# Four q turns moved from TensorE to DMA in an attention-and-MLP kernel

## The chip, the cores and the metric

The kernel runs on one core of one Trainium2 chip. The metric is the device time of one execution in microseconds, lower is better. It is about 1.8 us longer than the span of the profile of the same execution, which starts and ends with the first and last counted piece of work.

## The reference

Per batch and head there is a linear attention without softmax, then an RMS norm; then, over all heads together, a layer norm and a two-layer MLP with a residual.

```python
# 8 batches, 8 heads, 576 positions, head_dim 64; d_model 512, hidden 2048
kv  = np.einsum('bhsd,bhse->bhde', k, v)
out = np.einsum('bhsd,bhde->bhse', q, kv)
rms = np.sqrt(np.mean(out * out, axis=-1, keepdims=True) + 1e-06)
attn = out / rms * g_norm
x  = attn.transpose(0, 2, 1, 3).reshape(8, 576, 512)
xn = (x - mean(x)) / np.sqrt(var(x) + 1e-06) * g_ln
y  = x + np.maximum(xn @ w_ch1, 0.0) @ w_ch2
```

## The kernel before

The 8 x 576 rows are cut into tiles of 128 rows. Each batch has five slots: four of 128 rows, and a "last fifth" of 64 rows. A tile takes one slot (the last fifths of two batches share a tile). For every tile the kernel multiplies q by kv ("out"), and it reads q for that with head_dim on the partitions. So q has to be turned. There are two ways in the kernel. On TensorE a turn is four 128x128 identity matmuls and then one copy out of PSUM; as a DMA it is one transposing transfer on the SyncE (SP) queue. Before the change, all of batches 0 and 1 are turned on TensorE, and later batches by DMA, 20 blocks of 128x128 at a time.

```python
def q_turn_pe(b, t, h0, h1):                  # four blocks of slot t on TensorE
    # ... cut: tile and PSUM allocation
    for hp in range(h0 // 2, h1 // 2):
        nc.tensor.transpose(ps[:, hp, :],
            qp[b % 2][:, t, 2 * hp:2 * hp + 2, :].rearrange("p h d -> p (h d)"), identity)

def add_q_turn_pe(b, t, deps, key, eng, h0=0, h1=H):
    # ... plans the four transposes, then the copy from PSUM on VectorE or ScalarE

def q_turn_dma(b):                            # all 20 blocks of a batch
    att[b]["qT"] = work.tile([128, 20, 128], bf16, tag="qT", name="qT", bufs=3)
    nc.sync.dma_start_transpose(
        att[b]["qT"], qp[b % 2].rearrange("p t h d -> p (t h d)"))
```

The instructions are not written in the order of issue. Each step is put into a list with an engine, an estimated start and its dependences; a planner makes one order per engine from it, and each engine's instructions are put into the program in that order.

```python
# batch 1: q is copied into its turned-ready layout slot by slot on ScalarE, then turned
for t in range(5):
    # ... cut: key, and qperm = the ScalarE copy of slot t (t = 4 is loaded in place)
    add_q_turn_pe(1, t, [qperm, z1[1]], key + 1, ("DVE", "ACT")[t % 2])

# batch 2 and later: loads on GpSimd's queue, each behind a gate; then q copies (batch 2 alone) and a DMA turn
for t0, t1 in ((0, 2), (2, 4))[by_slot * 2:]:
    qperm.append(add("ACT", 0.85, 1.0, ok - 14, load["q", b][0:1] + [
        adone[b - 2]["qfree"]], lambda t0=t0, t1=t1: q_permute(nc.scalar, b, t0, t1)))
for x in kperm + qperm:
    x.lag = 4.0 if b == 2 else 6.0
turn = add_dma("SP", ok - 12, qperm + load["q", b] + (
    adone[b - 3].get("outs", []) if b >= 3 else []),
               lambda: q_turn_dma(b), 2.6e3, 1.0, occ=2.98, lat=0.25, tail=0.42)

# at the end: one order for all, and dummy matmuls in the early gaps of TensorE
order = run_plan()
# ... cut: idle[id(s)] = how many dummy matmuls go before TensorE step s
for s in order:
    if id(s) in idle:
        idle_mm(idle[id(s)])
    s.fn()
```

Three more names are used below. A "gate" is a one-column copy on GpSimd ("mark" in the profile) that reads a finished tile; the loads behind it in GpSimd's queue are issued after it (in the kernel before, one gate starts at 66.19 us, when the tile that it waits for has landed, and the load behind it at 66.65). "xT" is the normalized tile turned on TensorE and copied out of PSUM by ScalarE; the MLP's first layer ("m1") of a tile reads it. A "store" writes a finished tile of 256 KB to DRAM on the SP queue.

## Time and profile before

| | before |
|---|---|
| device time | 294.95 us, median of 3 (294.86 to 295.4) |
| PE busy | 283.4 us, 96% of the span |
| chain that ended last | on PE without a break from 25.53 to 290.36 us |
| q turns on PE that the change will remove | 4, of 0.22 us each |

These are the span, the busy times of the engines (with their number of instructions), and the chain by engine, from the page of the kernel before:

```profile
span 294.0 us, 5183 instructions
PE 283.4 (96%) x2061; PEld 161.6 (55%) x2061; DVE 166.1 (57%) x360; ACT 143.3 (49%) x288; POOL 65.5 (22%) x92
PE 90%; DMA 7%; POOL 1%; issue 1%; DVE 0%; POOLq 0%
```

TensorE (PE) is the bound: nine tenths of the chain are PE, and what the other engines do costs nothing as long as PE needn't wait for it. These are the four turns in question in the chain in order of time of the kernel before (start in us, length in us, what; the links between them are left out):

```profile
44.03 0.22 PE qT_ps L401 x4
47.07 0.22 PE qT_ps L401 x4
48.16 0.22 PE qT_ps L401 x4
52.05 0.22 PE qT_ps L401 x4
```

Each turn is a link of the chain, so each costs its 0.22 us in full. The next lines are from the DMA view of the kernel before for 36 to 52 us. The first has the queue, its packets, the MB moved and the share of the 16 engines' time; the others have the issues, with KB each and the median us from issue to landing.

```profile
q0 software_dynamic: 6651, 3.07, 146.9%
vb<-in_v_dram POOLq DMA_DIRECT2D x1, 512.0 KB, 14.1
qb<-in_q_dram POOLq DMA_DIRECT2D x1, 512.0 KB, 11.7
```

The loads keep the engines full throughout these 16 us. The q load of batch 2 ("qb") lands 11.7 us after its issue. Last, the timeline of the kernel before around this place (start, length, engine, line, what; in brackets idle time before it, and what ended it):

```profile
35.59 1.50 PE L429 MATMUL kv_ps<-vb,kp 96*128 96x128 bf16 x24
50.92 3.50 SPq L630 DMA_DIRECT2D out_dram<-x  x4
59.06 2.00 ACT L381 COPY qp<-qb 128x1024 bf16<-128x1024 bf16 x2
61.13 3.14 SPq L421 DMA_TRANSPOSE qT<-qp  x1
66.19 0.26 POOL L695 COPY mark<-qT 128x1 bf16<-128x1 bf16 x1 [9.32 <-DMA qT<-qp]
85.33 2.75 PE L598 MATMUL mm_ps<-xT,w 128*128 128x512 bf16 x12
```

ScalarE copies batch 2's q at 59.06 us without waiting (the load landed at 53.9). SP issues the DMA turn at 61.13, and GpSimd's one-column copy "mark", which waits for that turn only, starts at 66.19: about 5 us from issue to landing.

The first and last of these lines bound what I call the **stretch** below: from the start of batch 1's kv matmuls (35.59) to the first of the MLP's first-layer matmuls that is 128x512 (85.33; up to there they are 128x128), 49.74 us here. I call what follows block 2. All that the change adds to the DMA queues or takes from TensorE lies inside the stretch; of the rest of the change, the stores that are no longer split and batch 3's kv come later.

### The profile page before, as it was taken

Reading aid. Unit: us, or ns where it says so; the run is one execution under the profiler, and the core shown is the slowest. Engines: PE = TensorE matmul, PEld = TensorE weight load, DVE = VectorE, ACT = ScalarE, POOL = GpSimd, SP = SyncE. Lnnn points to the kernel's source line nnn. Section 1 sums busy time; section 2 is a strip of 40 time slices with the busy share of each in tenths; the row PEclk is TensorE's granted clock in tenths of the full one; section 3 lists DMA queues with packets and bytes.
Section 4 is the critical chain, followed back from the end, with each engine's and each line's share of the span. In section 5 each row is a group of like instructions: output and inputs, shape, how many; then the busy total and the mean of one; then the engine's idle time right before and its main releaser. Section 6 shows DMA issues by size and latency. Waiting matters only on the chain.

```text
span 294.0 us, 5183 instructions
## 1 busy us (share of the span) xinstructions
PE 283.4 (96%) x2061; PEld 161.6 (55%) x2061; DVE 166.1 (57%) x360; ACT 143.3 (49%) x288; POOL 65.5 (22%) x92
## 2 busy tenths in 40 slices
PE   3989999999999999999999999999999999999995
PEld 1879955977745445444544445444554444444444
DVE  1597048759876886557755775577557755420022
ACT  3268972987856612671267127611761177017400
POOL 8973230208209005403042316000000000000000
PEclk9999999999999999999999999999999999999999
DMA  7999999649989998991999699932201310220012
GB/s 98 181 199 205 203 199 192 173 91 108 189 173 95 167 132 159 174 212 56 171 116 146 115 142 133 178 96 89 56 18 54 91 54 18 56 85 22 0 74 73
DMA packets 107388, 35.21 MB, mean 120 GB/s; under 512 B 85603, under 2 KB 103395, under 8 KB 107364
## 3 DMA queue, kind: packets, MB, share of 16 engines
q0 software_dynamic: 72608, 18.35, 64.2%
q1 hardware_dynamic: 34516, 16.39, 23.6%
q8 instruction: 16, 0.26, 0.4%
q10 hardware_dynamic: 240, 0.13, 0.2%
q14 instruction: 8, 0.07, 0.1%
HBM read 36.70 MB, written 9.44 MB: 157 GB/s over the span
## 4 chain that ended last, share of the span: by engine, by line
PE 90%; DMA 7%; POOL 1%; issue 1%; DVE 0%; POOLq 0%
PE mm_ps L617 42%; PE mm_ps L598 33%; PE mm_ps L583 8%; DMA w<-in_moe_w_ch_dram 5%; PE kv_ps L429 3%; PE out_ps L452 3%; DMA vb<-in_v_dram 3%; PE xT_ps L533 1%; POOL kb L233 1%; PE qT_ps L401 0%; POOL vb L233 0%; DVE x L624 0%; POOL qp L254 0%; POOLq L943 0%
## 5 line engine op out<-in xcount | busy, mean ns | idle before, releaser
L617 PE MATMUL mm_ps<-w,m 128*128 128x512 bf16 (+2 forms) x608 | 130.3, 368 | 0.0
L598 PE MATMUL mm_ps<-xT,w 128*128 128x512 bf16 x448 | 100.8, 379 | 0.0
L605 ACT ACTIVATE m<-mm_ps 128x512 bf16<-128x512 f32 x112 | 66.8, 598 | 50.2 <-PE mm_ps L598 49.3
L617 PEld LDWEIGHTS <-m 128*128 128x128 bf16 x608 | 57.0, 98 | 59.6
L598 PEld LDWEIGHTS <-w 128*128 128x128 bf16 x448 | 43.1, 98 | 48.6
L624 DVE SCALAR_TENSOR_TENSOR x<-mm_ps,rstd,x 128x512 f32<-128x512 f32 (+2 forms) x38 | 27.3, 721 | 42.1 <-PE mm_ps L617 42.0
L474 DVE TENSOR_REDUCE ss<-sq 128x8 f32<-128x512 f32 (+1 forms) x37 | 24.8, 670 | 45.3 <-ACT sq L465 45.3
L465 ACT ACTIVATE sq<-out_ps 128x512 f32<-128x512 f32 (+1 forms) x37 | 21.5, 585 | 50.9 <-PE out_ps L452 50.9
L583 PE MATMUL mm_ps<-xT,w 128*128 128x128 bf16 x512 | 30.9, 219 | 0.7 <-ACT xT L540 0.7
L583 PEld LDWEIGHTS <-w 128*128 128x128 bf16 x512 | 29.3, 98 | 1.7 <-issue 0.8
L526 DVE SCALAR_TENSOR_TENSOR xc<-x,mv,gl 128x512 bf16<-128x512 f32 (+1 forms) x37 | 27.1, 736 | 1.1
L469 DVE TENSOR_TENSOR xg<-out_ps,gn 128x512 f32<-128x512 f32 (+1 forms) x37 | 24.8, 669 | 0.3
L691 POOL COPY mark<-xT 128x1 bf16<-128x1 bf16 x15 | 6.3, 423 | 64.2 <-DMA xT<-xc 55.4
L590 ACT ACTIVATE m<-mm_ps 128x512 bf16<-128x512 f32 x32 | 18.3, 598 | 2.8 <-PE mm_ps L583 2.2
L504 DVE TENSOR_TENSOR x<-xg,inv 128x512 f32<-128x512 f32 x24 | 16.6, 692 | 0.8
L520 DVE BATCH_NORM_STATS2 stats<-x 128x6 f32<-128x512 f32 x24 | 16.6, 690 | 0.5
L478 ACT ACTIVATE rms<-ss,eps_attn 128x8 f32<-128x8 f32 (+1 forms) x37 | 11.1, 300 | 10.0 <-DVE ss L474 9.9
L452 PEld LDWEIGHTS <-qT 128*128 128x128 bf16 x160 | 11.5, 98 | 7.1 <-DVE kv_pack L444 0.3
L444 DVE CAST kv_pack<-kv_ps 64x256 bf16<-64x256 f32 (+1 forms) x18 | 7.1, 392 | 14.8 <-PE kv_ps L429 14.5
L452 PE MATMUL out_ps<-kv_pack,qT 128*128 128x128 bf16 x160 | 15.0, 220 | 0.1
L429 PE MATMUL kv_ps<-vb,kp 128*128 128x128 bf16 (+1 forms) x144 | 11.7, 234 | 3.1 <-DMA vb<-in_v_dram 3.1
L429 PEld LDWEIGHTS <-kp 128*128 128x128 bf16 (+1 forms) x168 | 11.1, 105 | 4.6 <-DVE kp L383 2.0
(61 smaller groups left out, 175.2 us busy)
## 6 DMA issues: line engine op xcount, KB each, us to landing
out_dram<-x SPq DMA_DIRECT2D x28, 256.0 KB, 2.5
w<-in_moe_w_ch_dram POOLq DMA_DIRECT2D x8, 512.0 KB, 13.0
vb<-in_v_dram POOLq DMA_DIRECT2D x6, 512.0 KB, 10.2
kp<-in_k_dram POOLq DMA_DIRECT2D x5, 512.0 KB, 8.5
qp<-in_q_dram POOLq DMA_DIRECT2D x5, 512.0 KB, 9.3
out_dram<-x SPq DMA_DIRECT2D x14, 128.0 KB, 2.6
qb<-in_q_dram POOLq DMA_DIRECT2D x2, 512.0 KB, 15.9
qp<-in_q_dram POOLq DMA_DIRECT2D x10, 64.0 KB, 7.5
```

What stands on the lines that cost most here:

```text
L429: nc.tensor.matmul(ps[:, hp, :], lhsT=kp[b % 2][p, t, 2 * hp:2 * hp + 2, :].rearrange("p h d -> p (h d)"), rhs=(v5[b % 2][:, 2 * hp:2 * hp ...
L452: nc.tensor.matmul(o3[:, hp, :], lhsT=att[b]["qT"][:, 4 * t + hp, :], rhs=kv_pack[b % 3][:, hp, :], start=(i == 0), stop=(i == len(bs) - 1))
L465: nc.scalar.activation(sq[:, h0:h1, :], st[n]["ps", h0][:, h0:h1, :], func=AF.Square)
L469: nc.vector.tensor_mul(xg[:, h0:h1, :], st[n]["ps", h0][:, h0:h1, :], gn.to_broadcast([128, h1 - h0, D]))
L474: nc.vector.tensor_reduce(ss[:, h0:h1, :], st[n]["sq"][:, h0:h1, :], axis=AX.X, op=ALU.add)
L526: nc.vector.scalar_tensor_tensor(xc[:, f0:f1], in0=st[n]["x"][:, f0:f1], scalar=blk[m]["mv"][:, i, 0:1], in1=gl[:, f0:f1], op0=ALU.subtrac ...
L583: nc.tensor.matmul(ps[:, d, :], lhsT=w1[c][:, kk, d * 128:(d + 1) * 128], rhs=blk[m]["xT"][:, kk, i * 128:(i + 1) * 128], start=(kk == 0), ...
L590: nc.scalar.activation(st[n]["m1"][:, c, :, :], st[n]["m1ps", c], func=AF.Relu)
L598: nc.tensor.matmul(ps, lhsT=w1[c][:, kk, d * 128:(d + 1) * 128], rhs=blk[m]["xT"][:, kk, :], start=(kk == 0), stop=(kk == nKm - 1))
L605: nc.scalar.activation(blk[m]["m1", c][:, d, :], blk[m]["m1ps", g], func=AF.Relu)
L617: nc.tensor.matmul(st[n]["m2ps", f0], lhsT=m1_piece(n, c, d), rhs=w2[c][:, d, f0:f1], start=(c == 0 and d == 0), stop=(c == 3 and d == 3))
L624: nc.vector.scalar_tensor_tensor(x[:, f0:f1], in0=st[n]["m2ps", f0], scalar=blk[m]["rstd"][:, i, :], in1=x[:, f0:f1], op0=ALU.mult, op1=AL ...
```

## The change

Its intent: take four q turns (batch 1's slots 2, 3 and 4 and batch 0's slot 4) off the engine that bounds the kernel and give them to DMA, as the later batches have it. In words it was also said to let the loads of later batches go one tile sooner; no gate is moved in the diff, and GpSimd's queue stays the same instruction for instruction.

```diff
-    SPLIT_STORE = (21, 23, 25, 28)
+    SPLIT_STORE = (25,)
@@
-    def q_turn_dma(b):
-        att[b]["qT"] = work.tile([128, 20, 128], bf16, tag="qT", name="qT", bufs=3)
+    def q_turn_dma(b, t0=0, t1=5):
+        if "qT" not in att[b]:
+            att[b]["qT"] = work.tile([128, 20, 128], bf16, tag="qT", name="qT", bufs=3)
         nc.sync.dma_start_transpose(
-            att[b]["qT"], qp[b % 2].rearrange("p t h d -> p (t h d)"))
+            att[b]["qT"][:, 4 * t0:4 * t1, :],
+            qp[b % 2][:, t0:t1, :, :].rearrange("p t h d -> p (t h d)"))
+
+    def add_q_turn_dma(b, t0, t1, deps, key):
+        s = add_dma("SP", key, deps, lambda: q_turn_dma(b, t0, t1), 520.0 * (t1 - t0), 1.0,
+                    occ=0.6 * (t1 - t0) + 0.1, lat=0.25, tail=0.42)
+        for t in range(t0, t1):
+            adone[b].setdefault(("qT", t), []).append(s)
@@
-    add_q_turn_pe(0, 4, load["q", 0, 4] + [z1[0]], pos[8] - 50, "DVE")
+    add_q_turn_dma(0, 4, 5, load["q", 0, 4] + [z1[0]], pos[8] - 41)
@@
-                add_q_turn_pe(1, t, [qperm, z1[1]], key + 1, ("DVE", "ACT")[t % 2])
+                if t < 2:
+                    add_q_turn_pe(1, t, [qperm, z1[1]], key + 1, ("DVE", "ACT")[t % 2])
+                elif t > 2:
+                    add_q_turn_dma(1, *((2, 4) if t == 3 else (4, 5)), [qperm, z1[1]], key + 1)
```

The planner also re-orders: the outs of tiles 6 and 7 stand together, 8 us later for tile 6; the out of batch 2's slot 0 stands beside that of slot 1; batch 3's kv comes 8 matmuls later.

## The prediction

> **What bounds the kernel now.** TensorE. The busy table gives PE 283.4 us of a 294.0 us span (96%), and the chain of waits that ended last stays on PE without a break from 25.53 to 290.36 us. Before that it is loads, after it one VectorE write and a store. The granted clock is 0.999. So every PE instruction in that stretch costs its issue time; work on ScalarE (49%), VectorE (57%) or the queues costs nothing unless PE comes to wait for it.
>
> **What the change does, in the order of instructions.** PE loses 16 weight loads and 16 identity matmuls: four q turns. VectorE loses three 128x512 copies (0.42 us each), ScalarE one (0.58 us). The SP queue gains three DMA transposes of 8, 4 and 4 blocks, ahead of the first store; three stores are no longer split. The re-plan moves work: the outs of batch 1's slots 2 and 3 (tiles 6, 7) now stand together after the second group of tile 4's first layer (tile 6's was about 8 us earlier); batch 2's slot 0 joins slot 1; batch 3's kv comes 8 matmuls later. The GpSimd queue is unchanged row for row, and the diff moves no gate; of "one tile sooner" I see only that batch 2's last-fifth q load now waits for a DMA turn instead of the PE turn that held it to 52.58 us.
>
> **Cost.** Each q turn holds PE for 0.22 us in the chain (those at 43.87, 46.91, 47.99, 51.89 us). Removed: 4 x 0.22 = 0.9 us. All other PE work keeps its count.
>
> **Does PE wait for the new turns?** In the trace a 20-block q turn holds SP 3.1 to 5.1 us and lands 4.9 to 6.1 us after issue; a 4-block turn holds it 1.2 us and lands after 2.5. By blocks I estimate 3 to 4 us to landing for 8. The q copies of batch 1 end at 41.2 us and SP is idle until 50.9, so I expect slots 2 and 3 at 44 to 47 us, both fifths by 50; the readers stand at about 54 and 60.5 us. The DMA engines are full from 36 to 52 us (stretch table: mean share 1.3 to 1.6). [...] The 16 blocks delay batch 2's v and q loads by an estimated 2.6 us (20 blocks took 3.2 us at 62 to 66 us); they are read from 59 us on.
>
> The tight spot is tile 6: out at 54 instead of 45.8 us, first layer at about 65. The same steps of tile 4 took about 8.5 us (41.9 to 50.8), so 2 to 3 us are left. Batch 2's q copies stand behind three more evictions, so its turn and batch 3's loads should go up to 1 us later; the plan moved batch 3's kv to match.
>
> **Prediction: 294.1 us**, range 293.5 to 295.2. Faster by over 2%: 0.5%; within 2%: 98.5%; slower by over 2%: 1%.
>
> **What would show it.** PE busy down about 0.9 us; 16 fewer matmuls; no PE idle between 40 and 92 us; later stages all 0.9 us sooner; turns landing before 54 us.
>
> **What would make it wrong.** PE waiting at tile 6's or 7's out (a turn under load over 10 us), at their xT, or at batch 3's kv and outs because its loads go later; each wait adds directly. The unsplit stores should cost nothing: none is among the last tiles.

The turns needn't wait for the whole backlog of loads: that was my assumption. 294.95 us, the median before, less 0.9 us for the four turns and with no wait added, is 294.05, put as 294.1 us.

## The result, and the profile after

Ratios here and below are the mean time of one kernel's fast runs over that of the other's of the same rounds, so they aren't quite the ratios of the medians quoted.

| | before | changed |
|---|---|---|
| device time, median of 6 (lowest to highest) | 295.19 us (294.86 to 296.0) | 295.38 us (294.52 to 295.93) |
| ratio to before, 95% interval | | 1.0002 (0.9983 to 1.0021) |
| PE busy | 283.4 us | 282.3 us |
| the stretch | 85.33 - 35.59 = 49.74 us | 84.87 - 35.12 = 49.75 us |

The prediction of 294.1 us missed, and its range up to 295.2 us missed by 0.18 us. Page of the changed kernel, the lines as shown of before:

```profile
span 293.8 us, 5156 instructions
PE 282.3 (96%) x2045; PEld 160.3 (55%) x2045; DVE 164.9 (56%) x357; ACT 142.6 (49%) x287; POOL 66.0 (22%) x92
PE 75%; DMA 18%; POOL 3%; ACT 1%; issue 1%; DVE 0%; POOLq 0%
```

The 16 matmuls and 1.1 us of PE's busy time (0.9 us by the chain) are gone, as intended. But the chain is no longer PE's alone: DMA has 18% of it. Here is the changed kernel's chain, at the place where it returns to PE:

```profile
41.61 19.59 DMA qb<-in_q_dram
...
62.17 1.04 ACT qp L381
63.21 0.03 ACT sq L473
63.23 6.50 DMA qT<-qp
69.73 0.05 issue
69.78 0.62 PE out_ps L460 x8
```

Read from the bottom up: an out of batch 2 on PE waited for a DMA turn, issued at 63.23; that waited for ScalarE's q copies; and those waited for batch 2's q load, issued at 41.61, which took 19.59 us. Here is the changed kernel's DMA view for 36 to 52 us:

```profile
q0 software_dynamic: 5032, 2.45, 117.7%
q1 hardware_dynamic: 1580, 0.39, 26.3%
vb<-in_v_dram POOLq DMA_DIRECT2D x1, 512.0 KB, 18.3
qb<-in_q_dram POOLq DMA_DIRECT2D x1, 512.0 KB, 19.6
qT<-qp SPq DMA_TRANSPOSE x3, 9.4
```

The loads on the software queue moved 2.45 MB where they moved 3.07 before. The turns, on the hardware queue, moved only 0.39 MB in it (0.52 MB, 16 blocks of 32 KB, until the last one landed). The q load takes 19.6 us instead of 11.7, and each new turn takes over 9 us to land. And the changed kernel's timeline:

```profile
35.12 1.51 PE L437 MATMUL kv_ps<-vb,kp 96*128 96x128 bf16 x24
40.74 6.75 SPq L422 DMA_TRANSPOSE qT<-qp  x3
49.56 3.15 SPq L638 DMA_DIRECT2D out_dram<-x  x4
61.22 1.99 ACT L381 COPY qp<-qb 128x1024 bf16<-128x1024 bf16 x2 [1.21 <-DMA qb<-in_q_dram]
62.72 1.89 PE L625 MATMUL mm_ps<-w,m 128*128 128x512 bf16 x8
63.23 3.11 SPq L422 DMA_TRANSPOSE qT<-qp  x1
64.08 0.59 ACT L548 COPY xT<-xT_ps 128x512 bf16<-128x512 bf16 x1
64.72 3.73 PE L591 MATMUL mm_ps<-xT,w 128*128 128x128 bf16 x64
68.29 1.03 PE L625 MATMUL mm_ps<-w,m 128*128 128x512 bf16 x4
69.78 0.62 PE L460 MATMUL out_ps<-kv_pack,qT 128*128 128x128 bf16 x8 [0.46 <-DMA qT<-qp]
84.87 4.48 PE L606 MATMUL mm_ps<-xT,w 128*128 128x512 bf16 x20
```

There are two waits of PE in it.

- **First wait, 0.28 us.** Eight 128x512 matmuls hold PE from 62.72 for 1.73 us as the chain has them (their ends in the timeline overlap what follows), so PE is free at 64.45. The first layer of tile 6 starts at 64.72. It needs the xT copy, which ScalarE started at 64.08 and which takes 0.59 us. The turn on PE that it copies had ended at 62.89; but ahead of it in ScalarE's order stand the q copies, which waited 1.21 us for the load and ran to 63.21, and two instructions from 63.11 to 64.19. ScalarE ran nothing else in those 1.21 us.
- **Second wait, 0.62 us.** PE would have gone on at 68.29 + 0.86 = 69.15 and starts the outs at 69.78, when batch 2's turn had landed.

0.28 + 0.62 = 0.90 us, against four turns of 0.224 us = 0.89 us saved. That is why the stretch is the same to 0.01 us. (The bracket says 0.46 where I count 0.62, since the modelled end of the matmuls before overlaps the wait. Where a wait is quoted from a bracket below, it can be too small in the same way.)

### The profile page after: what moved, and what is told of

Its sections match the earlier page's. It is cut to its first block, busy times and chain, and to the rows that moved or that the text cites. A ratio compares the mean times of both kernels' runs of the same rounds, so it can differ in the third digit from the quotient of the medians.

```text
span 293.8 us, 5156 instructions
## 1 busy us (share of the span) xinstructions
PE 282.3 (96%) x2045; PEld 160.3 (55%) x2045; DVE 164.9 (56%) x357; ACT 142.6 (49%) x287; POOL 66.0 (22%) x92
## 4 chain that ended last, share of the span: by engine, by line
PE 75%; DMA 18%; POOL 3%; ACT 1%; issue 1%; DVE 0%; POOLq 0%
PE mm_ps L625 36%; PE mm_ps L606 33%; DMA qb<-in_q_dram 13%; DMA kb<-in_k_dram 2%; PE out_ps L460 2%; DMA qT<-qp 2%; PE kv_ps L437 2%; PE mm_ps L591 1%; ACT qp L381 1%; POOL kb L233 1%; POOL w L334 1%; POOL w L336 0%; POOL vb L233 0%; PE xT_ps L541 0%; POOL qp L254 0%
## 5 line engine op out<-in xcount | busy, mean ns | idle before, releaser
L606 PEld LDWEIGHTS <-w 128*128 128x128 bf16 x448 | 43.1, 98 | 48.8
L632 DVE SCALAR_TENSOR_TENSOR x<-mm_ps,rstd,x 128x512 f32<-128x512 f32 (+2 forms) x38 | 27.4, 720 | 41.5 <-PE mm_ps L625 41.3
L702 POOL COPY mark<-xT 128x1 bf16<-128x1 bf16 x15 | 6.9, 458 | 56.0 <-DMA xT<-xc 53.5
L452 DVE CAST kv_pack<-kv_ps 64x256 bf16<-64x256 f32 (+1 forms) x18 | 7.1, 393 | 16.4 <-PE kv_ps L437 16.1
## 6 DMA issues: line engine op xcount, KB each, us to landing
qb<-in_q_dram POOLq DMA_DIRECT2D x2, 512.0 KB, 19.4
```

What stands on the lines that cost most here:

```text
L606: nc.tensor.matmul(ps, lhsT=w1[c][:, kk, d * 128:(d + 1) * 128], rhs=blk[m]["xT"][:, kk, :], start=(kk == 0), stop=(kk == nKm - 1))
L632: nc.vector.scalar_tensor_tensor(x[:, f0:f1], in0=st[n]["m2ps", f0], scalar=blk[m]["rstd"][:, i, :], in1=x[:, f0:f1], op0=ALU.mult, op1=AL ...
```

## The experiments

Each set of kernels ran beside the kernel before on the same chip; the medians of before that are quoted with a run are those of its own set. If nothing had to wait, the stretch of the changed order would be 49.74 - 0.89 = 48.85 us. This is the yardstick.

### Set 1: what delays the q load?

**e1: the turns' traffic alone.** The kernel before keeps its four PE turns and its order, and the same three DMA turns are issued in addition, into batch 2's buffer, where nobody reads them and batch 2's own turn overwrites them.

```diff
 # ... cut: spare_turn, a DMA turn into batch 2's buffer
+    spare_turn(0, 4, 5, 8, load["q", 0, 4] + [z1[0]], pos[8] - 41)   # 4 blocks
@@
                 add_q_turn_pe(1, t, [qperm, z1[1]], key + 1, ("DVE", "ACT")[t % 2])
+                if t > 2:   # 8 and 4 blocks into batch 2's buffer, before its own turn
+                    spare_turn(1, *((2, 4, 0) if t == 3 else (4, 5, 12)), [qperm, z1[1]], key + 1)
```

> The kernel before, every instruction in its old place, plus the three DMA turns (8, 4 and 4 blocks) of the change, written where nobody reads them. Theory C (contention: the turns' transfers hold up batch 2's q load, and with it batch 2's own turn): q load of batch 2 about 18 to 20 us to landing instead of 11.7; batch 2's turn starts at 63 us or later instead of 61.1; PE waits 1 to 2.5 us at the out matmuls of batch 2's slot 0, which stand at 67.8 us in this order; stretch from batch 1's kv matmuls to block 2's first first-layer matmul 50.7 to 52.3 us instead of 49.74; time 1 to 2.5 us longer than before. Rival O (the re-planned order is what costs, turns by DMA are free): time and stretch as before, within 0.3 us. Rival N (nothing is lost, noise hides a gain of 0.9): as before, within 0.3 us.

Measured: 296.44 us against 295.09, ratio 1.0055 (1.0024 to 1.0085); the stretch is 85.61 - 34.77 = 50.84 us, 1.1 us more; the q load took 19.5 us. The timeline of e1:

```profile
60.93 1.99 ACT L381 COPY qp<-qb 128x1024 bf16<-128x1024 bf16 x2 [2.57 <-DMA qb<-in_q_dram]
65.77 1.95 PE L594 MATMUL mm_ps<-xT,w 128*128 128x128 bf16 x32 [0.61 <-ACT xT L551]
```

So the traffic is enough to delay the load and to make PE wait, with no change of order at all. PE's order is that of before, so the start times of its matmuls can be laid side by side: PE loses 0.78 us at this xT and 0.31 us at the next outs, which together are the 1.1 us. I had expected the whole of it at the outs. (The stretch holds 1.10 of the 1.35 us between the medians; the rest lies outside it, and I did not trace it.)

**e2: the changed order without the traffic.** The DMA turns are planned but not issued, and their readers take a slot that is turned already. The result is wrong (relative error 0.38).

```diff
-        s = add_dma("SP", key, deps, lambda: q_turn_dma(b, t0, t1), 520.0 * (t1 - t0), 1.0,
+        s = add_dma("SP", key, deps, lambda: None, 520.0 * (t1 - t0), 1.0,
@@  # in t_out
-                    o3[:, hp, :], lhsT=att[b]["qT"][:, 4 * t + hp, :],
+                    o3[:, hp, :], lhsT=att[b]["qT"][:, 4 * (0 if (b, t) in (
+                        (1, 2), (1, 3), (1, 4), (0, 4)) else t) + hp, :],
```

> The changed kernel with the three DMA turns left out and everything else in its place; the outs that needed them read slot 0 instead, so the result is wrong on purpose. Theory C: no PE wait at batch 2's outs, q load of batch 2 lands in about 12 us, the stretch from batch 1's kv matmuls to block 2's first first-layer matmul falls from 49.75 to 48.8 us, time 0.7 to 1.0 us shorter than before (ratio about 0.997). Rival O (order): stretch stays at 49.7, time as before. Rival N: stretch and time as the changed kernel.

Measured: 294.44 us against 295.09, ratio 0.9975 (0.9962 to 0.9989); the q load took 11.7 us again; there is no wait at tile 6's first layer or at batch 2's outs. The stretch is 49.15 us, not the expected 48.8: laid beside e3 below, whose PE order is the same, the excess of 0.30 us stands at 40 to 42 us (0.21 of it is a wait at 41.86 us for the copy of a PE turn, which this change doesn't touch), and nothing is lost after that. The order is not at fault; the traffic is.

**e3: the changed kernel with its first stores later.** The stores of tiles 0 to 3 (1 MB) are issued at 49.56 us in the changed kernel. With the q load delayed, they now run beside it. Here they go behind batch 2's turn, and nothing else moves.

```diff
     order = run_plan()
+    late = [done[n]["store"] for n in range(4)]
+    order = [s for s in order if s not in late]
+    i = order.index(adone[2]["qT", 0][0]) + 1
+    order[i:i] = late
```

> The changed kernel with one thing moved: the stores of tiles 0 to 3 stand behind batch 2's turn on the SP queue, so that 1 MB of stores no longer shares the DMA engines with batch 2's q load. Theory C with the stores as the second part of the delay: q load of batch 2 lands at 56 to 58 us instead of 61.2, ScalarE does not wait for it, no PE wait at batch 2's outs, stretch 48.8 to 49.0 us, time 0.7 to 1.0 us shorter than before. If the turns' own transfers make the whole delay, the q load still lands after 60 us and the stretch stays at 49.6 or more.

Measured: 294.10 us against 295.09, ratio 0.9972 (0.9957 to 0.9986). The stretch is 83.64 - 34.79 = 48.85 us, the yardstick. From the timeline and the DMA view of e3:

```profile
59.58 1.98 ACT L381 COPY qp<-qb 128x1024 bf16<-128x1024 bf16 x2
64.12 3.74 PE L591 MATMUL mm_ps<-xT,w 128*128 128x128 bf16 x64
68.56 0.61 PE L460 MATMUL out_ps<-kv_pack,qT 128*128 128x128 bf16 x8
qb<-in_q_dram POOLq DMA_DIRECT2D x1, 512.0 KB, 15.8
```

No bracket is left: ScalarE and PE wait for nothing here. The q load still takes 15.8 us. So of the 7.9 us of delay, about 4.1 are the turns' alone (15.8 - 11.7), and about 3.8 more come from the stores that the delayed load runs into (19.6 - 15.8).

**e5: the unsplit stores alone.** The kernel before with only the first hunk of the diff.

```diff
-    SPLIT_STORE = (21, 23, 25, 28)
+    SPLIT_STORE = (25,)
```

> The kernel before with only the three stores unsplit; PE order unchanged. All theories: same time within 0.3 us, stretch 49.7 us. If it is slower by 0.5 us or more, the unsplit stores take part in the loss.

Measured: 295.27 us against 295.09, ratio 1.0005 (0.9993 to 1.0016); the stretch is 49.84 us. This hunk is free.

### Set 2: can the cost be avoided another way?

**a2: the changed kernel again, unedited.**

> The changed kernel again, unedited, as the reference of this call. Theory C: q load of batch 2 again 18 to 20 us to landing, PE again idle 0.6 to 1.2 us between batch 1's kv matmuls and block 2, stretch 49.5 to 50.1, time within 0.5 us of before. If this profile shows no PE wait there and a stretch near 48.9, the wait of the first profile was chance.

Measured: 294.63 us against 295.12, ratio 0.9985 (0.9972 to 0.9997); the stretch is 49.90 us and PE's wait at batch 2's outs 0.59 us in the bracket (0.46 in the first profile). The waits come back in another run.

**e4: tell the planner that batch 2's q lands later,** so that it puts ScalarE's q copies behind other work.

```diff
             for x in kperm + qperm:
                 x.lag = 4.0 if b == 2 else 6.0
+            if b == 2:
+                for x in qperm:
+                    x.lag = 8.0
```

> The changed kernel with one number of the planner raised: batch 2's two q copies are taken to be ready 8 us after the planner's estimate of the load instead of 4, so that these copies, batch 2's turn and batch 2's outs stand later in the queues. Transfers are unchanged. Theory C (the loss is a wait at places fixed too early, not bandwidth as such): q load of batch 2 still lands in 18 to 20 us, but nobody waits for it; stretch 48.8 to 49.2, time 0.6 to 0.9 us shorter than before. If the loss cannot be ordered away: stretch 49.6 or more, time as before.

Measured: 295.25 us against 295.12, ratio 1.0005 (0.9992 to 1.0018); the stretch is 84.46 - 34.77 = 49.69 us where I expected 48.8 to 49.2: a miss. The timeline of e4, at the start of block 2:

```profile
84.46 7.71 PE L606 MATMUL mm_ps<-xT,w 128*128 128x512 bf16 x35 [0.67 <-ACT xT L548]
```

The planner moved the turn back to 65.99 us and batch 2's outs to 72.47; the early wait went, and the tiles that were now late made PE wait 0.67 us here. With this one setting the wait was moved and not removed; I tried no other.

**e6: only slots 2 and 3 by DMA,** the two last fifths back on PE. 8 blocks of traffic instead of 16, 0.45 us saved on PE instead of 0.89.

```diff
-    add_q_turn_dma(0, 4, 5, load["q", 0, 4] + [z1[0]], pos[8] - 41)
+    add_q_turn_pe(0, 4, load["q", 0, 4] + [z1[0]], pos[8] - 50, "DVE")
@@
-                if t < 2:
+                if t < 2 or t == 4:
```

> Only batch 1's slots 2 and 3 by DMA (8 blocks); both fifths on PE again. Theory C: half the blocks, so q load of batch 2 lands 2 to 4 us after where it lands before (53.9), at about 56 to 58 us plus what the stores add, hardly later than the copies that read it; two PE turns saved, so stretch 49.3 (0.45 less), time 0.2 to 0.6 us shorter than before. A wait of over 0.3 us here would say that even 8 blocks are too many beside this load.

Measured: 294.56 us against 295.12, ratio 0.9980 (0.9968 to 0.9992); the stretch is 49.40 us (49.3 expected); the q load took 16.9 us and PE waited at neither place. Half of the turns give half of the saving, and it is kept all but 0.1 us, with the stores in their old place. The 8-block turn still took 9.2 us to land.

**e8: e1 with its stores late.**

```diff
  # the kernel of e1, and the edit of e3
```

> The kernel before plus the three spare DMA turns, as in the first experiment, and with the stores of tiles 0 to 3 behind batch 2's turn. Theory C with two parts (turns add about 4 us to the q load, the stores another 4): q load of batch 2 about 16 us to landing, at 57 us, before the copies that read it stand at 59; no new PE wait; stretch 49.6 to 49.9; time within 0.4 us of before. If the turns alone are enough for the loss: stretch 50.5 or more and time over 0.8 us longer.

Measured: 295.53 us against 295.12, ratio 1.0011 (0.9999 to 1.0023); the q load took 15.4 us, with no later wait of PE. The stretch is 50.12 us, above the expected 49.6 to 49.9, because 0.57 us of waits stand at its start, at 39 to 41 us (0.19, 0.17 and 0.21), for q copies that come before the edit has done anything; about 0.2 us of such waits are in the kernel before too. The load's time is as it was in e3: about 15.5 us with turns and without stores, in two different orders.

### Set 3: repeat, and hold the loads back

**e3b and a3: the kernels of e3 and a2 again, on another chip.**

> The version with the first four stores behind batch 2's turn again, now in one call with the changed kernel, to see whether it beats both. Theory C: stretch 48.8 to 48.9, no PE wait at batch 2's outs, time 0.7 to 1.0 us shorter than before and at least 0.4 us shorter than the changed kernel.

> The changed kernel unedited, beside the version with late stores. Stretch 49.7 to 50.0, PE wait of 0.6 us at batch 2's outs, time between 0.6 us shorter than before and the same.

Measured, against 295.58 us of the kernel before: e3b 294.65 us, ratio 0.9968 (0.9954 to 0.9982), stretch 48.85 us, q load 16.4 us; a3 295.56 us, ratio 0.9997 (0.9983 to 1.0011), stretch 49.72 us, q load 20.0 us, PE's wait at batch 2's outs 0.56 us in the bracket.

**e9: are the new turns slow because the loads run beside them?** Batch 2's v and q loads are held until the last new turn has landed.

```diff
     order = run_plan()
+    turns = [adone[1]["qT", 2][0], adone[0]["qT", 4][0], adone[1]["qT", 4][0]]
+    at = max(order.index(t) for t in turns)
+    held = [s for s in order[order.index(load["v", 2][0]):at] if s.eng == "POOL"]
+    order = [s for s in order if s not in held]
+    at = max(order.index(t) for t in turns) + 1
+    # ... cut: gate = a new step on GpSimd
+    gate.fn = lambda: nc.gpsimd.tensor_copy(mark, att[1]["qT"][:, 16, 0:1])
+    order[at:at] = [gate] + held
```

> The changed kernel with batch 2's v load, and all loads behind it, held until the last of the three new turns has landed (a small GpSimd copy that reads it, as the later gates do); nothing else moves. Between 41 and 47 us the turns then share the DMA engines with one 512 KB load instead of two or three. For the time to landing of the first turn (8 blocks), 9.2 to 9.8 us so far: if the load beside it makes it slow, 4 to 6.5 us; if it is slow by itself or by the chain of three, 8.5 us or more. Batch 2's v load goes about 10 us later, so its kv matmuls, at 60.5 us, will make PE wait: time longer by 1 to 5 us, which is not the point of the run.

Measured, one run of unknown state: 296.84 us, stretch 50.81 us. The first turn took 9.5 us, as before; of the other two the median was 6.2 us instead of 9.3 or 9.4. But the engines weren't idle beside the first: earlier loads still kept them full (from 41.5 to 50 us the software queue moved 0.90 MB, a share of 99%). So this experiment is inconclusive for the first turn; for the other two it agrees that they land sooner beside less traffic. Holding the loads is no remedy: PE waited 1.19 us at tile 6's first layer and 0.45 us at the outs (brackets), though not at batch 2's kv matmuls, where I had expected it.

### Sets 4 and 5: why batch 2's turn lands after 6.6 us, not 5.0

The second wait is the larger one, and it isn't explained by the late start of the turn alone. In before that turn was issued at 61.13 us and landed after 5.0; in the changed kernel it was issued 2.1 us later and took 6.6; with 5.0 it would have landed at 68.2, ahead of the 69.15 us at which PE was free for the outs. The records of single packets in the trace show how. In them this turn gives 16 completions. In the changed kernel 15 of them came by 68.14 us, and the last at 69.73. In before, and in e1 to e6 and e8, all 16 of this turn came within 0.2 us of each other.

I had two suspects: the store of tile 4, which SP issues at 67.02 us right behind the turn, and a fetch of 16 KB of instructions, whose packet in the changed kernel started at 67.66 us, as the turn's data ended. There are 16 such fetches in the run (the queue "instruction" on the page has 16 packets and 0.26 MB), one for about every 128 of its 2045 matmuls on average.

**e10: the store of tile 4 behind that of tile 5.** e10b is the same kernel once more, run because e10's profile fell on its fastest execution.

```diff
     order = run_plan()
+    four, five = done[4]["store"], done[5]["store"]
+    order.remove(four)
+    order.insert(order.index(five) + 1, four)
```

> The changed kernel with one store moved: tile 4's, issued 3.8 us after batch 2's turn in the changed kernel, goes behind tile 5's, about 7 us later. In all three profiles of the changed kernel 15 of the 16 completions of that turn come within 0.14 us of each other, 4.9 us after its issue, and the sixteenth 1.6 us later; in between lie a 16 KB instruction fetch and this store. Theory S (the store beside the turn's tail makes the sixteenth late): turn lands in 5.0 us, no PE wait at batch 2's outs, only the 0.28 us at tile 6's transposed input stays; stretch about 49.15, time 0.4 to 0.8 us shorter than before. Theory F (the instruction fetch makes it late, the store only happens to stand there): turn still lands 5.5 to 6.6 us after issue, PE wait 0.1 to 0.6 us, stretch 49.3 to 49.75. Under both the q load still lands in 19 to 20 us and ScalarE still waits 1.2 us for it.

> The kernel with tile 4's store later, once more, because its profile was of its fastest execution (294.14 us; the others 295.2 to 296.2). A usual execution should show ScalarE waiting 1.2 us for batch 2's q, the sixteenth completion 1.6 us late again although no store is near, and PE waiting 0.3 to 0.6 us at batch 2's outs; stretch 49.4 to 49.8.

Measured, e10: 295.57 us (294.14 to 296.18) against 295.57, ratio 1.0006 (0.9991 to 1.0022). In its profiled execution, the stretch was 48.85 us, as the q load landed a little sooner (18.4 us); but the last completion of the turn came at 68.58 us, 1.6 us behind the others, with no store there. (PE was free for the outs at 68.80 us only, so it didn't wait: a late completion costs nothing when the load comes this little sooner.) e10b, one run of unknown state: 295.34 us, stretch 49.69. Here is e10b's DMA view for 66 to 71 us in 40 equal slices (busy share of the engines in tenths; a packet is counted where it starts), one line of the same view for 67.9 to 71 us, and then its timeline for PE and GpSimd:

```profile
DMA  9999999999999340000000000000000000000000
```

```profile
q1 hardware_dynamic: 2, 0.00, 0.1%
```

```profile
69.90 0.62 PE L460 MATMUL out_ps<-kv_pack,qT 128*128 128x128 bf16 x8 [0.46 <-DMA qT<-qp]
69.97 0.19 POOL L706 COPY mark<-qT 128x1 bf16<-128x1 bf16 x1 [14.63 <-DMA qT<-qp]
```

Slice 15 ends at 66 + 15 x 0.125 = 67.9 us. From there on no data packet starts, of a turn, a load or a store; and yet PE and GpSimd get the turn only at 69.9. The turn's last data packet had ended at 67.80, 15 completions came by 68.27, and one was missing until 69.86. The store is ruled out. The two packets that are left are the key. By the packet records, each such turn is closed by 32 packets of 4 bytes. Here 30 of them had started by 67.77, as the data ended; the last two started at 68.66 and 68.67, just as the packet of the instruction fetch (67.80 to 68.68) ended.

**e11 and e12: move the instruction fetch.** There are dummy matmuls in TensorE's gaps ahead of its first main matmuls. I left out 40 (e11) or 20 (e12) of them, so that the fetch would meet a later point of the work, while nothing in the stretch changes. That a fetch moves with the matmuls was my assumption, from the average alone. Counted from the start of tile 6's first layer on PE, the fetch came after 2.94 us in the changed kernel, 4.25 in e11 and 2.77 in e12: later in e11, not in e12. Counted from the issue of batch 2's turn, it came after 4.43, 6.79 and 4.25 us.

```diff
+    for at in (4, 5, 6):          # e12: (5,)
+        idle[list(idle)[at]] = 0
     for s in order:
         if id(s) in idle:
```

> The changed kernel with 40 of the 73 idle warm-up matmuls before 18 us left out; nothing else changes. The 16 KB instruction fetches come on average every 128 matmuls, [...]; with 80 fewer instructions ahead, the fetch that met the end of batch 2's turn is asked for about 40 matmuls (2.2 us) later, after the turn has landed. Theory F (this fetch makes the sixteenth completion late): all 16 completions within 0.3 us, turn lands about 5.0 us after issue, no or little PE wait at batch 2's outs; the 0.3 us at tile 6 stays; stretch 49.0 to 49.3. Rival R (the late completion belongs to the turn and its queue): sixteenth again 1.6 us late, stretch 49.6 to 49.9. [...]

> As the run before, with only 20 idle matmuls left out: the fetch is asked for about 1.1 us later, which is still inside the turn's transfer (64.4 to 67.6 us). Theory F: sixteenth completion late as in the changed kernel (1 to 1.7 us). Rival R: the same. If it is not late here but is in the run with 40, both are wrong.

Measured, e11: 295.47 us against 295.55, ratio 0.9997 (0.9975 to 1.0018); the stretch is 84.91 - 36.06 = 48.85 us. First the instruction queue in the changed kernel's DMA view for 67 to 69 us:

```profile
q8 instruction: 1, 0.02, 2.7%
```

In e11's view of the same 2 us that queue has no line: its fetch is now at 69.64 us. And these are lines of e11's timeline:

```profile
62.85 3.08 SPq L422 DMA_TRANSPOSE qT<-qp  x1
67.83 0.65 POOL L706 COPY mark<-qT 128x1 bf16<-128x1 bf16 x1 [11.93 <-DMA qT<-qp]
69.83 0.61 PE L460 MATMUL out_ps<-kv_pack,qT 128*128 128x128 bf16 x8
```

The turn lands 67.83 - 62.85 = 4.98 us after its issue: with the fetch moved away, no completion is late. That PE doesn't wait and that the stretch is 48.85 us is not shown to come from it. With fewer dummy matmuls the stretch started at 36.06 us instead of 35.12, while the loads went as before, so the q load (18.7 us) landed 24.4 us after the start of the stretch instead of 26.1, ScalarE didn't wait for it, and a turn 1.6 us longer would still have landed before PE was free for the outs at 69.83. For the same reason the time of e11 is no shorter: the later start ate the gain.

e12, one run of unknown state: 294.39 us, stretch 49.32. Its fetch was at 67.33 us, while the turn was still moving; I had expected the completion to be late there too, and it was not (4.98 us from issue to landing). These are lines of e12's timeline:

```profile
61.06 1.99 ACT L381 COPY qp<-qb 128x1024 bf16<-128x1024 bf16 x2 [1.10 <-DMA qb<-in_q_dram]
68.06 0.27 POOL L706 COPY mark<-qT 128x1 bf16<-128x1 bf16 x1 [12.22 <-DMA qT<-qp]
69.00 0.61 PE L460 MATMUL out_ps<-kv_pack,qT 128*128 128x128 bf16 x8
```

This is the run that separates the two waits: q is as late as in the changed kernel, the completion is on time, PE loses 0.16 us at tile 6's xT and nothing at the outs. (The rest of its 0.47 us over the yardstick stands at 40 to 42 us, as in e2.) So a fetch inside the turn isn't enough. In every run with the late completion (the changed kernel, a2, a3, e9, e10, e10b) the fetch started within 0.01 us before the end of the turn's last data packet, the last two of the 32 closing packets started within 0.02 us before the end of the fetch's packet, 0.88 to 0.93 us later, and the last completion came 1.09 to 1.19 us after that end. In all other runs all 32 started by the end of the data or within 0.02 us of it, also where a fetch started 0.03 to 0.04 us before that end (e1, e2, e6).

The same can be looked for in every transposing transfer of the 17 profiles. Of 550, 12 have a last completion that is over 1 us (1.5 to 2.0) behind the fifteenth, one of them in the kernel before (issued at 251.51 us). Beside each of the 12 a fetch started within 0.16 us of the end of the other data, and the last completion came 1.03 to 1.19 us after the end of the fetch's packet. The records don't name the engine of a packet, so where the late part of the transfer waited is not shown.

### All runs in one table

| run | edit | ratio to before (95%) | stretch, us | q load, us | last completion late? |
|---|---|---|---|---|---|
| before | | 1 | 49.74 | 11.7 | no |
| changed | | 1.0002 (0.9983-1.0021) | 49.75 | 19.6 | yes |
| a2, a3 | changed again | 0.9985 (0.9972-0.9997), 0.9997 (0.9983-1.0011) | 49.90, 49.72 | 19.6, 20.0 | yes |
| e1 | before + turns | 1.0055 (1.0024-1.0085) | 50.84 | 19.5 | no |
| e2 | changed, no turns | 0.9975 (0.9962-0.9989) | 49.15 | 11.7 | no |
| e3, e3b | changed, stores late | 0.9972 (0.9957-0.9986), 0.9968 (0.9954-0.9982) | 48.85, 48.85 | 15.8, 16.4 | no |
| e4 | changed, plan q later | 1.0005 (0.9992-1.0018) | 49.69 | 19.5 | no |
| e5 | before, stores unsplit | 1.0005 (0.9993-1.0016) | 49.84 | 11.7 | no |
| e6 | changed, 8 blocks only | 0.9980 (0.9968-0.9992) | 49.40 | 16.9 | no |
| e8 | e1, stores late | 1.0011 (0.9999-1.0023) | 50.12 | 15.4 | no |
| e9 | changed, loads held | one run | 50.81 | 8.8 | yes |
| e10, e10b | changed, store 4 late | 1.0006 (0.9991-1.0022), one run | 48.85, 49.69 | 18.4, 19.4 | yes |
| e11 | changed, 40 fewer dummies | 0.9997 (0.9975-1.0018) | 48.85 | 18.7 | no |
| e12 | changed, 20 fewer dummies | one run | 49.32 | 19.2 | no |

How sharp the edge was can be read from all profiles of the changed order. Laid beside e3, which never waits, PE's start times give the first wait of each run. In six profiles (changed, a2, a3, e9, e10b, e12) it is the time by which the q load landed later than 25.8 us after the start of the stretch (25.96 to 27.16 us, waits of 0.15 to 1.35 us; for e12 the 0.31 us lost earlier are taken off). In e10 (25.02 us) and e11 (24.36 us) nothing waited. In before it landed at 18.28 us. So of the 7.8 us by which the changed kernel's load landed later against PE's clock, 7.5 were free and 0.27 were paid: either half of the delay alone lies inside that margin. An execution whose load lands a little sooner keeps the gain, as e10's fastest did; that this is why the executions of the changed kernel spread from 294.26 to 295.93 us is likely, but not shown.

e3 is the version that beats both kernels: the kernel before by 0.3% in two sets on two chips, and the changed kernel by 0.3% in the set where both ran, with a correct result. (What counts here is whether the interval contains 1.) That is the 294.1 / 294.95 = 0.9971 that the prediction had promised for the change itself.

## Why the prediction was wrong

- **The saving: right.** "Removed: 4 x 0.22 = 0.9 us." PE busy fell by 1.1 us, matmuls by 16, and in e3, where nothing waits, the stretch fell from 49.74 to 48.85 us.
- **The new turns' readers: right, for a wrong reason.** The outs at 53.18 and 60.07 us had no wait; the turns landed at 50.6, 53.3 and 54.9 us. But "3 to 4 us to landing for 8" was 9.8 us, and "both fifths by 50" was 54.9. A turn's time was taken from places with idle DMA engines; beside a full software queue it took two and a half to three times as long as estimated. The trace of the kernel before had shown it: its 24 turns of 4 blocks landed after 2.4 us at the least, 2.5 in the median and 7.6 at the most, and the one of 7.6 us (issued at 95.82) stands beside loads. That the turns needn't wait for the whole backlog held so far: the first turn, issued at 40.74 us, landed at 50.6, ahead of the v load, which was issued at 36.19 and landed at 54.5; but it took those 9.8 us.
- **The step that failed:** "The 16 blocks delay batch 2's v and q loads by an estimated 2.6 us (20 blocks took 3.2 us at 62 to 66 us); they are read from 59 us on." The v load was delayed by 4.2 us and the q load by 7.9. Two terms were mis-sized. First, the turns alone cost the q load 3.7 to 4.7 us and not 2.6 (e3, 15.8 us, e8, 15.4 us, and e3b, 16.4 us, against 11.7): what the turns take from full engines beside loads is more than they take alone. Second, the sum had no term for what a delayed load runs into next: four stores of 256 KB at 49.56 us, which in before came when the load had only 3 us to go, cost 3.8 us more (19.6 to 15.8, e3). That made q land at 61.2 us, past its first reader's place in ScalarE's order, and past 35.12 + 25.8 = 60.9 us, from which on PE feels it.
- **What "Batch 2's q copies stand behind three more evictions, so its turn … up to 1 us later" missed.** The delay came from the load, and the turn was 2.1 us later. By ScalarE's order a wait for batch 2's data (1.21 us) then stood ahead of tile 6's xT, which has nothing to do with batch 2: PE's first wait, 0.28 us. I had named this wait ("at their xT") as what could make the prediction wrong, without a size.
- **"No PE idle between 40 and 92 us; later stages all 0.9 us sooner": false.** PE waited 0.28 and 0.62 us. The second needs the late load and, besides, the last completion of batch 2's turn 1.6 us late (e12: the load as late, completion on time, no wait at the outs; e10: the completion late, the load less so, no wait either). The prediction had no term for this completion; where a fetch falls beside a turn was nobody's plan, and with 20 dummy matmuls fewer (e12) it fell 4.25 instead of 4.43 us after the turn's issue, with no late completion.
- **The unsplit stores: right.** e5, 1.0005.
- **The base.** The range was laid around 294.95 us; the kernel before gave medians of 295.09 to 295.58 us in later sets. The unedited changed kernel gave 295.38, 294.63 and 295.56. A 0.3% effect can be judged by ratios in the same rounds only.

Shown: the traffic of the turns causes it (e1 with it, e2 without it); the stores carry half of the delay, and moving them wins the saving back (e3, e3b); the late completion isn't the store's doing (e10b), was absent in both runs whose fetch came at another moment of the turn (e11, e12), and by the packet records goes with closing packets that start only as the fetch's packet ends (six runs of six). That it costs 0.62 us at the outs when the load is late too rests on e12, one run of unknown state, against three profiles of the changed kernel and e10b. Open: why the fetch gets in between data and closing packets in some runs and not in e1, e2 and e6, and why the last completion then comes 1.1 to 1.2 us after its packets, where the others take about 0.5.

## What to carry to other kernels

A transfer's time must be taken from a stretch with the same DMA load as the place where it is to go (here a turn of 4 blocks landed after 2.5 us in the median before, and after 9.1 and 9.4 us beside the loads), and a load that it delays must be followed to the next transfers that it will then overlap: here the second collision cost as much as the first. Ask how much lateness the reader can bear: here 7.5 us were free, and the next 0.3 us were paid in full. Look at what stands behind each new wait in its engine's order: here ScalarE's wait of 1.21 us for q stood ahead of a copy that the bounding engine needed, and cost it 0.28 us; in e3, with no such wait, the moved work was free. When DMA traffic is added at a full place, look for transfers that nobody waits for, such as stores, and let those go later; moving four stores kept the whole gain.

## What was measured of turns, loads and fetches

- 4-block turns took 2.5 us to landing in the kernel before (median of 24), and 9.1 and 9.4 us beside the loads in the changed kernel; the q load lost 3.7 to 4.7 us to 16 blocks whose size is 0.52 MB.
- Of the four 128x128 matmuls of a turn on TensorE, one held it for 0.224 / 4 = 0.056 us; twenty blocks by DMA moved in 3.2 us, 0.16 us each, and landed 5.0 us after issue (batch 2's turn in the kernel before).
- Batch 2's turn alone on the engines moved 188 to 224 GB/s in the full slices of the kernel before's DMA view for 62 to 70 us; a plain store in the same view reached 358 to 410.
- Where the packet of a fetch of 16 KB of instructions (0.88 to 0.93 us) came between the data and the closing packets of batch 2's turn, one of the 16 completions came 1.6 us late (six runs of six); over all profiles it was 12 of 550 transposing transfers, by 1.5 to 2.0 us.
